# Fused linear attention and squared-ReLU MLP: sums by a product in the first steps, a new order, a last tile in parts

## The chip, the cores and the metric

The kernel runs on one core of a Trainium2 chip. The metric is the time of one execution on the device in microseconds (us); smaller is better. The time before is the median of three runs. A profile is one execution recorded by the hardware profiler; its span runs from the first to the last instruction of the program, and the time of that same execution is a little longer than its span.

Engines: PE is the matrix engine, PEld its weight loads, DVE the vector engine, ACT the scalar engine, POOL the general engine, SP the engine that issues DMAs. "Line" with L and a number is the line of the kernel in the profile of before; the changed kernel has its code eight lines or so further down.

## The reference

Two parts follow each other. The first is a recurrence over 768 positions for 4 batches and 8 heads of 48 columns. The state is a 48x48 matrix for each batch and head.

```python
for t in range(S):
    cur = np.einsum('bhd,bhe->bhde', u[None] * kt, vt)
    y[:, :, t] = np.einsum('bhd,bhde->bhe', rt, state + cur)
    state = wt[:, :, :, None] * state + np.einsum('bhd,bhe->bhde', kt, vt)
```

The second takes the result as 3072 rows of 384 columns and computes `relu(x @ w_in) ** 2 @ w_out`, with 2048 columns in the middle. The output is 3072x384 in float32.

## The kernel before, in words

The 768 positions of a batch are cut into 6 chunks of 128, so there are 24 steps (4 batches of 6 chunks). A step works on all 8 heads, 384 columns, of one chunk. Within a chunk the recurrence becomes products: r is multiplied by the decay up to its position, k by the inverse of the decay, and the products of k and r under a triangular mask replace the loop. Only the state goes from chunk to chunk.

The kernel is written as small functions, one per piece of work, and each has a short name. For step s they are, in the order of the data:

- `ld:s:w`, `ld:s:r`, `ld:s:k`, `ld:s:v` load the chunk (192 KB each, SP, L150).
- `lw` takes the logarithm of w (ACT, L246). `cum` sums it down the chunk by a product with a strict triangle (PE, L272). `ci` makes the inclusive sum with its sign turned, from the exclusive one and lw (DVE, L276). `exp` takes both to the exponent (ACT, L283). `rd` multiplies r and k by them (DVE, L293). The tile of `cum` is in a ring of one buffer (`cp`), which `p` uses too from step 3 on.
- `tr` transposes r and k (PE, L302), `rkt` copies the result to SBUF (DVE or ACT, L187), `p` multiplies k with r (PE, L321), `pm0` and `pm1` mask the two halves (DVE, L333), `ye` multiplies with v into y (PE, L381).
- `su` forms the chunk's own share of the state and the total decay (PE, L347 and L351), `ac` takes the decay's exponent (ACT, L289), `ts` adds the old state (DVE, L356), `sn` applies the decay and gives the new state (DVE or POOL, L190). `ys` multiplies the state with r into y (PE, L370). Where a step has `su` but no `ts`, `sn` reads the product's tile itself. A set `by_product`, empty in this kernel, names steps in which `su` adds the old state by a product with the identity.
- `ku`, `qp`, `q`, `vq` are the term with u (POOL or DVE, L190, with a sum on DVE, L262). `ysb` adds it to y (DVE, L386). `yt` transposes y (PE, L394), `xt` copies it as x to SBUF (ACT or DVE, L187).

`tr`, `su` and `yt` share one buffer (`tr`) in PSUM, so each waits until the copy out of the one before is done.

The second part works on 17 blocks of rows: 0 to 8 of one step (128 rows), 9 to 15 of two steps (256 rows), 16 of one. `m1:i:g` is a group of 12 products (128 columns wide) or 6 products (256 wide) of block i (PE, L412), into a ring of two buffers. `rl` is the ReLU of a group (ACT, L421, or DVE, L423) and `gt` its square: from the ReLU's result by ACT (L433) or DVE (L435), or, with the letter W, by DVE from the PSUM tile and the ReLU (L430), in which case the buffer is free only after `gt`. `m2:i:mt:q` is a quarter of the second product of a 128-row tile (4 products, PE, L454), `os` copies the tile out (L461, L463), `store` writes it (192 KB, SP, L467). The very last tile is split in columns 0 to 255 and 256 to 383 (L450), copied out by `oh` on ACT (L479) and DVE (L480), and written by `sh` with one DMA from ACT's queue (L484) and one from SP's (L485).

The two weights come in four groups each (`ld:g:i`, `ld:g:o`, 768 KB, L176 and L182), and `cast` turns the parts of a group to bfloat16 on ACT, POOL or DVE (L187). `warm` gives PE products on zeros where it has nothing else to do (L473).

What sets the order is a table of words, `ORDER` (lines 16 to 98). The kernel walks it once, and each word issues its instructions. An engine runs its own instructions in exactly that order, and a wait of one holds all behind it on the same engine; a letter at a word's end (A, V, G) names the engine that does it. SP issues the loads and stores in the table's order too. The DMAs finish nearly in the order of issue.

Of the kernel before, what the change touches and what calls it, by code (L numbers as in the profile page):

```python
# [21 lines left out]
warm:1:1 ci:3 vq:2:G yt:0 ysb:1 p:2 exp:3 v:2:V ku:3:G ys:2 pm0:2 xt:0:A warm:1 rd:3 yt:1 cast:i:0:2:A
warm:3:1 qp:3:G xt:1:A pm1:2 cast:i:0:0:A tr:3 q:3 cast:i:0:1:A ye:2 rkt:3:V m1:0:0 cast:i:1:0:G cast:i:1:1:A
ysb:2 m1:1:0 cast:i:1:2:G rl:0:0:A su:2 gt:0:0:W rl:1:0:A ld:4:k p:3 ac:2 pm0:3 cast:i:2:1:G m1:0:1
cast:i:2:2:A ts:2 gt:1:0:A m1:1:1 cast:i:2:0:V sn:2:G rl:0:1:A pm1:3 yt:2 m1:1:2 rl:1:1:V cast:i:3:0:A
cast:i:3:1:G ys:3 gt:0:1:V rl:1:2:A m1:0:2 cast:i:3:2:G gt:1:1:A xt:2:V ld:4:w m1:2:0 rl:0:2:A cast:o:0:2:V
# [5 lines left out]
rl:3:2:A m1:3:3 ld:5:k rkt:4:V gt:3:2:A m2:1:0:2 cast:o:3:0:G cast:o:3:3:A rl:3:3:V ld:6:w cast:o:3:2:A ys:4
cast:o:3:1:G p:4 gt:3:1:V gt:3:3:A m2:0:0:2 ld:7:w pm0:4 lw:5 m2:0:0:3 pm1:4 v:4:G ld:6:r m2:1:0:3 os:0:0:A
vq:4:G cum:5 ye:4 ld:6:k os:1:0:A ci:5 su:4 m2:2:0:0 ac:4 ysb:4 exp:5 ku:5:G ld:8:w ts:4 m2:2:0:1 sn:4:V yt:4
qp:5:G m2:3:0:0 ld:7:r xt:4:A rd:5 m2:2:0:2 store:0:0 q:5 m2:2:0:3 ld:7:k m1:4:0 ld:5:v os:2:0:A lw:6 m1:4:1
rl:4:0:V ld:6:v lw:7 cum:6 tr:5 rl:4:1:A ci:6 m1:4:2 ld:8:r gt:4:0:A rkt:5:V m1:4:3 exp:6 gt:4:1:V ku:6:G
m2:3:0:1 rl:4:2:A rd:6 ld:7:v rl:4:3:A m2:4:0:0 qp:6:G gt:4:2:A p:5 ld:8:v ys:5 gt:4:3:A pm0:5 m2:4:0:1 v:5:A
vq:5:G ld:8:k pm1:5 tr:6 lw:8 q:6 ye:5 cum:7 rkt:6:A ld:9:r m2:4:0:2 ysb:5 ku:7:G ci:7 m2:3:0:2 ld:9:k qp:7:G
exp:7 yt:5 m2:3:0:3 xt:5:V ld:9:w rd:7 v:6:A vq:6:G m1:5:0 os:3:0:A su:6 ld:10:r q:7 rl:5:0:A p:6 m1:5:1 ac:6
pm0:6 gt:5:0:A ld:10:k v:7:G sn:6 m1:5:3 rl:5:1:A pm1:6 vq:7:G ld:10:w tr:7 gt:5:1:A v:8:V m2:5:0:0 rl:5:3:A  # L40
rkt:7:V store:1:0 m1:5:2 ku:8:G gt:5:3:A ld:9:v ye:6 ld:11:r rl:5:2:A cum:8 m2:4:0:3 qp:8:G ysb:6 gt:5:2:A
ci:8 yt:6 ld:11:k m2:5:0:1 ku:9:G xt:6:V exp:8 q:8 ys:7 m1:6:0 ld:10:v lw:9 vq:8:G rd:8 su:7 rl:6:0:A m1:6:1
qp:9:V ac:7 p:7 gt:6:0:A ts:7 ld:12:r m2:5:0:2 rl:6:1:A pm0:7 ku:10:G os:4:0:A m1:6:3 ld:12:k q:9 gt:6:1:A
sn:7:G pm1:7 m1:6:2 rl:6:3:A ld:13:r tr:8 qp:10:G lw:10 gt:6:3:W ye:7 rl:6:2:A cum:9 store:2:0 m2:5:0:3 ysb:7
vq:9:G rkt:8:A store:3:0 ci:9 m2:6:0:0 ld:13:k q:10 gt:6:2:A ys:8 v:9:V yt:7 m2:6:0:1 exp:9 ld:11:w ku:11:V
m2:6:0:2 xt:7:A rd:9 qp:11:G ld:12:w m1:7:0 v:10:A ld:11:v vq:10:G su:8 q:11 rl:7:0:A p:8 m1:7:2 ac:8 pm0:8
gt:7:0:A pm1:8 ku:12:G m1:7:1 ld:14:r os:5:0:A rl:7:2:A ts:8 m2:6:0:3 qp:12:G rl:7:1:V ld:14:k gt:7:2:A cum:10
ye:8 os:6:0:V tr:9 gt:7:1:A sn:8:G store:4:0 ysb:8 m1:7:3 rkt:9:A ld:13:w ci:10 m2:7:0:0 q:12 ld:14:w rl:7:3:A
yt:8 ku:13:V m2:7:0:1 exp:10 gt:7:3:W ld:12:v qp:13:G m2:7:0:2 xt:8:A rd:10 lw:11 m2:7:0:3 ld:15:r q:13 su:9
cum:11 ac:9 m1:8:0 v:11:G ci:11 lw:12 ld:15:k ts:9 m1:8:2 exp:11 vq:11:G os:7:0:V tr:10 rl:8:0:A ld:13:v  # L50
sn:9:G rd:11 ys:9 rkt:10:A m1:8:1 ku:14:V ld:16:r p:9 rl:8:2:A su:10 qp:14:G pm0:9 gt:8:0:A m1:8:3 ld:16:k
pm1:9 ac:10 m2:8:0:0 rl:8:1:A ts:10 ld:15:w gt:8:2:A ye:9 q:14 sn:10:G p:10 gt:8:1:A ysb:9 tr:11 store:5:0
rl:8:3:A pm0:10 ld:16:w m2:8:0:1 vq:12:G lw:13 pm1:10 ld:17:r m2:8:0:2 gt:8:3:A rkt:11:V lw:14 cum:12 ys:10
# [47 lines left out]
def kernel(  # L101
# [11 lines left out]
    nc = tc.nc  # L113
# [414 lines left out]
```

## Time and profile before

| what | value |
| --- | --- |
| time, median of 3 runs | 194.65 us (194.36 to 194.76) |
| the profiled execution | 194.57 us, span 192.8 us |
| PE busy | 183.3 us (95%) |
| DVE busy | 158.5 us (82%) |
| ACT busy | 141.4 us (73%) |
| POOL busy | 80.9 us (42%) |
| memory traffic | 25.17 MB read, 4.72 MB written |
| shares of the chain that ended last | PE 77%, SP's queue 6%, DVE 5%, ACT 4%, DMA 4% |

The chain is followed back from the last instruction, at each step to what released it. Busy time of PE is modelled, since products are pipelined: a product counts as busy until its result is out, so that short waits can lie within it.

### The profile page before, as it was taken

Reading aid. Unit: us, or ns where it says so; the run is one execution under the profiler, and the core shown is the slowest. Engines: PE = TensorE matmul, PEld = TensorE weight load, DVE = VectorE, ACT = ScalarE, POOL = GpSimd, SP = SyncE. Lnnn points to the kernel's source line nnn. Section 1 sums busy time; section 2 is a strip of 40 time slices with the busy share of each in tenths; the row PEclk is TensorE's granted clock in tenths of the full one; section 3 lists DMA queues with packets and bytes.
Section 4 is the critical chain, followed back from the end, with each engine's and each line's share of the span. In section 5 each row is a group of like instructions: output and inputs, shape, how many; then the busy total and the mean of one; then the engine's idle time right before and its main releaser. Section 6 shows DMA issues by size and latency. Waiting matters only on the chain.

```text
span 192.8 us, 5428 instructions
## 1 busy us (share of the span) xinstructions
PE 183.3 (95%) x2171; PEld 138.4 (72%) x2171; DVE 158.5 (82%) x289; ACT 141.4 (73%) x283; POOL 80.9 (42%) x107
## 2 busy tenths in 40 slices
PE   7799699999999999999999999999999999999993
PEld 2345488777777877877778678768768778778772
DVE  4599787987788989899999999998877987877540
ACT  3555689875989989897978666859969858726440
POOL 5287564355397765575366359162141300000000
PEclk9999999999999999999999999999999999999999
DMA  6999998999899999999989899602002000111012
GB/s 133 213 209 274 364 321 194 377 190 219 188 215 185 206 230 183 225 200 233 236 186 216 190 211 226 175 4 82 0 3 82 3 26 19 43 44 41 0 44 82
DMA packets 107180, 30.24 MB, mean 157 GB/s; under 512 B 100370, under 2 KB 105619, under 8 KB 107155
## 3 DMA queue, kind: packets, MB, share of 16 engines
q1 hardware_dynamic: 107010, 29.76, 65.9%
q8 instruction: 17, 0.28, 0.6%
q10 hardware_dynamic: 144, 0.13, 0.2%
q14 instruction: 9, 0.07, 0.1%
HBM read 25.17 MB, written 4.72 MB: 155 GB/s over the span
## 4 chain that ended last, share of the span: by engine, by line
PE 77%; SPq 6%; DVE 5%; ACT 4%; DMA 4%; issue 1%; ACTq 0%
PE m L454 30%; PE m L412 29%; SPq L150 6%; PE tr L302 4%; DMA w_st<-in_moe_w_in_dram 4%; PE cp L321 3%; PE y L381 2%; PE tr L394 2%; PE tr L347 2%; ACT rl L421 2%; PE cp L272 1%; PE y L370 1%; DVE rl L423 1%; PE m L450 1%; DVE gt L435 1%
## 5 line engine op out<-in xcount | busy, mean ns | idle before, releaser
L412 PE MATMUL m<-xT,wi_sb 128*128 128x128 bf16 (+1 forms) x816 | 73.9, 241 | 1.6 <-ACT rl L421 0.3
L454 PE MATMUL m<-wo_sb,gt 128*128 128x384 bf16 x368 | 70.3, 326 | 0.0
L412 PEld LDWEIGHTS <-wi_sb 128*128 128x128 bf16 x816 | 59.8, 97 | 10.0 <-issue 1.7
L421 ACT ACTIVATE rl<-m 128x512 f16<-128x512 f32 x73 | 42.4, 595 | 10.8 <-PE m L412 10.1
L454 PEld LDWEIGHTS <-gt 128*128 128x128 bf16 x368 | 33.4, 97 | 16.9
L433 ACT ACTIVATE gt<-rl 128x512 bf16<-128x512 f16 x57 | 35.3, 631 | 3.8 <-DVE rl L423 3.2
L190 POOL TENSOR_TENSOR qprod<-rk_raw,ku 128x384 f32<-128x384 f32 x23 | 23.5, 1024 | 17.9 <-DVE ku L190 13.1
L333 DVE TENSOR_TENSOR pmT<-cp,tri_strict 128x512 bf16<-128x512 f32 x42 | 27.4, 684 | 4.2 <-PE cp L321 3.9
L293 DVE TENSOR_TENSOR rdec_buf<-rk_raw,cp 128x768 bf16<-128x768 f32 x24 | 22.8, 950 | 3.3 <-ACT cp L283 2.9
L190 POOL TENSOR_TENSOR vq<-v_raw,q 128x384 f32<-128x384 f32 x21 | 17.5, 837 | 13.1 <-DVE y_sb L386 6.5
L283 ACT ACTIVATE cp<-cp 128x768 f32<-128x768 f32 x24 | 19.2, 800 | 3.4 <-DVE cp L276 3.1
L190 POOL TENSOR_TENSOR ku<-rk_raw,u_bc 128x384 f32<-128x384 f32 x17 | 17.3, 1019 | 5.7 <-DMA rk_raw<-in_k_dram 5.7
L423 DVE TENSOR_SCALAR rl<-m 128x512 f16<-128x512 f32 x23 | 15.6, 686 | 3.9 <-PE m L412 3.6
L435 DVE TENSOR_TENSOR gt<-rl 128x512 bf16<-128x512 f16 x34 | 16.3, 481 | 2.9 <-ACT rl L421 2.5
L190 POOL TENSOR_TENSOR S<-t_state,ac_buf 128x384 bf16<-128x384 f32 x12 | 10.2, 848 | 17.1 <-DVE t_state L356 13.1
L276 DVE SCALAR_TENSOR_TENSOR cp<-cp,lw_buf 128x384 f32<-128x384 f32 x24 | 13.4, 559 | 4.2 <-PE cp L272 4.0
L302 PE MATMUL tr<-ident,rdec_buf 128*128 128x128 bf16 x192 | 14.7, 219 | 1.6 <-ACT xT L187 1.2
L461 ACT ACTIVATE o_sb<-m 128x384 f32<-128x384 f32 x18 | 8.8, 488 | 8.1 <-PE m L454 7.4
L386 DVE TENSOR_TENSOR y_sb<-vq,y 128x384 bf16<-128x384 f32 x24 | 13.1, 547 | 1.9 <-PE y L381 1.7
L302 PEld LDWEIGHTS <-rdec_buf 128*128 128x128 bf16 x192 | 12.1, 98 | 3.4 <-issue 1.6
L246 ACT ACTIVATE lw_buf<-w_raw 128x384 bf16<-128x384 f32 x24 | 12.3, 519 | 2.1 <-DMA w_raw<-in_w_dram 1.8
L262 DVE TENSOR_REDUCE q<-qprod 128x8 f32<-128x384 f32 x24 | 13.0, 544 | 0.1
(63 smaller groups left out, 212.9 us busy)
## 6 DMA issues: line engine op xcount, KB each, us to landing
w_raw<-in_w_dram SPq DMA_DIRECT2D x24, 192.0 KB, 3.8
rk_raw<-in_r_dram SPq DMA_DIRECT2D x24, 192.0 KB, 3.8
rk_raw<-in_k_dram SPq DMA_DIRECT2D x24, 192.0 KB, 3.7
v_raw<-in_v_dram SPq DMA_DIRECT2D x24, 192.0 KB, 3.9
out_dram<-o_sb SPq DMA_DIRECT2D x23, 192.0 KB, 2.6
w_st<-in_moe_w_in_dram SPq DMA_DIRECT2D x4, 768.0 KB, 8.7
w_st<-in_moe_w_out_dram SPq DMA_DIRECT2D x4, 768.0 KB, 7.1
out_dram<-o_sb ACTq DMA_DIRECT2D x1, 128.0 KB, 1.9
```

The costliest lines, as they stand in the source:

```text
L190: {"V": nc.vector, "G": nc.gpsimd}[eng].tensor_mul(dst, a, b)
L276: nc.vector.scalar_tensor_tensor(out=cs[:, 1, 0:DM].rearrange("p (h d) -> p h d", h=H), in0=cs[:, 0, 0:DM].rearrange("p (h d) -> p h d", h ...
L283: nc.scalar.activation(cs[:, :, 0:DM], cs[:, :, 0:DM], AF.Exp)
L293: nc.vector.tensor_mul(rdec[:, :, :, 0:D], raw["rk", s][:], tiles.pop(("cs", s))[:, :, 0:DM].rearrange("p a (h d) -> p a h d", h=H))
L302: nc.tensor.transpose(ps_tr[:, i, p, :], rdec[:, i, 2 * p:2 * p + 2, :], ident[:])
L333: nc.vector.tensor_mul(tiles["pmT", s][:, e], tiles["p", s][e].rearrange("p (a t) -> p a t", a=HP), tri_strict[:, None, :].to_broadcast([C ...
L412: nc.tensor.matmul(ps1[:, j, :], wi_sb[:, kk, n * 128:(n + 1) * 128], xT[:, kk, s0 * C:s0 * C + width], start=(kk == 0), stop=(kk == KT - 1))
L421: nc.scalar.activation(rl[:], m1[:], AF.Relu, scale=RS)
L423: nc.vector.tensor_scalar(rl[:], m1[:], RS, 0.0, op0=ALU.mult, op1=ALU.max)
L433: nc.scalar.activation(gt, rl[:], AF.Square)
L435: nc.vector.tensor_mul(gt, rl[:], rl[:])
L454: nc.tensor.matmul(tiles["m2", i, mt][:], gt[:, n, mt * 128:(mt + 1) * 128], wo_sb[:, n, :], start=(n == 0), stop=(n == NT - 1))
```

## The change

- **Sums.** In steps 0, 1 and 2 `cum` makes the inclusive sum by a second product, with a triangle of -1 that has its diagonal (`tri_neg`, built by POOL at the start). The words `ci:0`, `ci:1` and `ci:2` are gone.
- **Old state.** `by_product` is now steps 1 and 2: `su` starts with a product of the identity and the old state, and `ts:1` and `ts:2` are gone; `sn` reads the product's tile.
- **Order.** The table is written anew from the first loads to the end. Other engines do some of the work: of 96 ReLUs DVE does 20 (before 23), of 96 squares DVE does 40 (39; 9 of them from PSUM, before 5), of 24 copies of `rkt` 10 (15), of 23 output copies 12 (5), of 28 casts ACT does 10 (12). Of the 24 `qp` DVE does 5 (1), of the 24 `ku` 5 (7).
- **Fillers.** `warm` uses a zero tile of 128 columns, read four times instead of a tile of 256 read twice; a filler still has 512 columns. There are 32 of them and 5 half ones (35 and 6).
- **Last tile.** Its second half does columns 0 to 255 of all middle rows first and then columns 256 to 383, where before the two parts alternated until the last quarter. Both of its stores go through SP.

The diff without most of the table:

```diff
 ORDER = """
...
-ld:1:k warm:1:1 uc:A v:0:A tr:0 ku:0:V ld:2:k warm:2 qp:0:G lw:1 rkt:0:V ld:1:v cum:1 lw:2 su:0 ci:1 p:0 ac:0
...
-ld:18:r ye:10 ci:12 ku:15:G v:12:A yt:9 m2:8:0:3 ysb:10 xt:9:A ld:14:v exp:12 qp:15:G yt:10 ys:11 xt:10:V
-v:13:A rd:12 m1:9:0 vq:13:G os:8:0:A ld:17:k m1:9:3 q:15 rl:9:0:A ku:16:V tr:12 rl:9:3:A ld:19:r gt:9:0:V p:11
...
+ld:1:k warm:1:1 uc:A v:0:A tr:0 ku:0:V ld:2:k warm:2 qp:0:G lw:1 rkt:0:V ld:1:v cum:1 lw:2 su:0 q:0 p:0 exp:1
...
+m2:8:0:1 ld:17:k ac:10 ci:11 vq:12:G v:12:A m2:8:0:2 ts:10 exp:11 ld:14:v q:15 sn:10:G yt:10 m2:8:0:3 lw:12
+xt:10:V rd:11 ld:15:w m1:9:0 lw:13 m1:9:1 rl:9:0:V vq:13:G cum:12 os:8:0:V tr:11 ld:16:w rl:9:1:A v:13:G ci:12
...
     make_upper_triangular(nc, tri_strict[:], val=1.0, diag=False)
+    tri_neg = consts.tile([C, C], BF16)
+    make_upper_triangular(nc, tri_neg[:], val=-1.0, diag=True)
...
-    warm = consts.tile([C, 256], BF16)
+    warm = consts.tile([C, 128], BF16)
...
+    sum_by_product = frozenset([0, 1, 2])
+
     def cum_(s):
         lw = tiles["lw", s]
         cs = tiles["cs", s] = ps_cp.tile([C, 2, 512], FP32, name="cp")
         nc.tensor.matmul(cs[:, 0, 0:DM], tri_strict[:], lw[:, :, 0:D], start=True, stop=True)
+        if s in sum_by_product:
+            nc.tensor.matmul(cs[:, 1, 0:DM], tri_neg[:], lw[:, :, 0:D], start=True, stop=True)
...
-    by_product = frozenset([])
+    by_product = frozenset([1, 2])
...
-            ns = range(4 * q, 4 * q + 4)
-            for n, (t, lo, hi) in ([(n, x) for n in ns for x in parts] if q < 3 else
-                                   [(n, x) for x in parts for n in ns]):
+            pa, pb = parts
+            todo_n = {2: [(n, pa) for n in range(8, 12)],
+                      3: [(n, pa) for n in range(12, 16)] + [(n, pb) for n in range(8, 16)]}.get(
+                          q, [(n, x) for n in range(4 * q, 4 * q + 4) for x in parts])
+            for n, (t, lo, hi) in todo_n:
...
-        ps = ps_m1.tile([C, 2, 256], FP32, name="m1")
+        ps = ps_m1.tile([C, 4, 128], FP32, name="m1")
...
-        nc.scalar.dma_start(out=out[t0:t0 + C, 0:EA], in_=tiles.pop("oa")[:, 0:EA])
+        nc.sync.dma_start(out=out[t0:t0 + C, 0:EA], in_=tiles.pop("oa")[:, 0:EA])
         nc.sync.dma_start(out=out[t0:t0 + C, EA:DM], in_=tiles.pop("ob")[:, 0:DM - EA])
```

Two places of the new order follow as the engines get it. The first is SP's queue ahead of the first group of the first weight (`w_st`); `w_raw`, `rk_raw` and `v_raw` are the chunk's tiles, and the numbers tell the buffers apart. Before:

```order
L150 DMA v_raw_202<-in_v_dram 128x8x48
L150 DMA v_raw_231<-in_v_dram 128x8x48
L150 DMA w_raw_249<-in_w_dram 128x8x48
L150 DMA rk_raw_253<-in_r_dram 128x8x48
L150 DMA rk_raw_253<-in_k_dram 128x8x48
L176 DMA w_st_262<-in_moe_w_in_dram 128x3x512
```

and in the changed kernel:

```order
L150 DMA v_raw_207<-in_v_dram 128x8x48
L150 DMA v_raw_235<-in_v_dram 128x8x48
L150 DMA w_raw_250<-in_w_dram 128x8x48
L150 DMA v_raw_254<-in_v_dram 128x8x48
L150 DMA rk_raw_269<-in_r_dram 128x8x48
L150 DMA rk_raw_269<-in_k_dram 128x8x48
L176 DMA w_st_314<-in_moe_w_in_dram 128x3x512
```

The load of v of step 3 stood behind five groups of weights; now it stands ahead of all of them. ACT at the same place, where it casts the first weights; `xT` is the copy of x, `wi_sb` the cast weight. Before:

```order
L187 COPY xT_100<-tr_388 128x3x128
L187 CAST wi_sb_98<-w_st_262 128x512
L187 COPY xT_100<-tr_420 128x3x128
L187 CAST wi_sb_98<-w_st_262 128x512 x2
L187 CAST wi_sb_98<-w_st_327 128x512
```

and now:

```order
L187 COPY xT_100<-tr_407 128x3x128
L187 CAST wi_sb_98<-w_st_314 128x512 x2
L187 CAST wi_sb_98<-w_st_339 128x512 x2
L295 ACTIVATE ac_buf2_133<-tr_490 64x4 x2
L427 ACTIVATE rl_535<-m1_502 128x512
```

The copy of x of step 1 is now ahead of the casts and that of step 0 is DVE's; ACT casts two of the three parts of the first group, and POOL the third.

The second place is DVE in steps 1 and 2, where it works without a pause. Numbers with `pmT`'s inputs tell the steps apart. Before, from the mask of step 0 on:

```order
L333 TENSOR_TENSOR pmT<-m_217,tri_strict 128x512
L190 TENSOR_TENSOR S<-tr,ac_buf_124 128x384
L293 TENSOR_TENSOR rdec_buf_132<-rk_raw,cp 128x16x48
L333 TENSOR_TENSOR pmT<-m_218,tri_strict 128x512
L276 SCALAR_TENSOR_TENSOR cp<-cp,lw_buf_122 128x384
L187 COPY rkT<-tr 128x1024
L386 TENSOR_TENSOR y_sb<-vq,y 128x384
L293 TENSOR_TENSOR rdec_buf_134<-rk_raw,cp 128x16x48
```

and now:

```order
L339 TENSOR_TENSOR pmT<-m_224,tri_strict 128x512
L339 TENSOR_TENSOR pmT<-m_225,tri_strict 128x512
L299 TENSOR_TENSOR rdec_buf_137<-rk_raw,cp 128x16x48
L190 TENSOR_TENSOR S<-tr,ac_buf_129 128x384
L392 TENSOR_TENSOR y_sb<-vq,y 128x384
L190 TENSOR_TENSOR ku<-rk_raw,u_bc 128x384
L264 TENSOR_REDUCE q<-qprod 128x8
L190 TENSOR_TENSOR qprod<-rk_raw,ku 128x384
L299 TENSOR_TENSOR rdec_buf_139<-rk_raw,cp 128x16x48
```

Between the `rd` of step 1 (`rdec_buf_132`, now `rdec_buf_137`) and that of step 2 (`rdec_buf_134`, now `rdec_buf_139`) stood four instructions and now stand five others: a mask, `ci` and the copy `rkT` left, and `S`, `ku`, `q` and `qp` of steps 0 to 2 came.

More of the change, by code (lines that the diff above doesn't have):

```diff
@@ L22 @@
[L22 to L26, printed above, removed]
@@ L32 @@
[L32 to L36, printed above, removed]
@@ L37 @@
[L37 to L51, printed above, removed]
@@ new lines @@
+v:9:A vq:9:G m2:5:0:3 pm0:8 rl:7:0:A q:11 lw:11 su:9 m1:7:1 gt:7:0:A pm1:8 ld:11:v m1:7:2 ac:9 ku:12:G
+os:5:0:V rl:7:1:A ld:15:r ts:9 cum:10 ye:8 rl:7:2:A m2:7:0:0 ci:10 qp:12:G v:10:A ld:15:k gt:7:1:V tr:9
+gt:7:2:A sn:9:G m1:7:3 ysb:8 exp:10 store:3:0 vq:10:V m2:7:0:1 store:4:0 rkt:9:A rd:10 ld:16:r m2:6:0:3
+ku:13:G rl:7:3:A m2:7:0:2 q:12 ld:12:v gt:7:3:A qp:13:V yt:8 p:9 xt:8:A m2:7:0:3 q:13 ld:12:w ku:14:G pm0:9
+tr:10 ld:13:w pm1:9 m1:8:0 v:11:A vq:11:G os:7:0:V rkt:10:A m1:8:1 qp:14:G rl:8:0:V ld:13:v ys:9 ye:9 rl:8:1:A
```

130 lines of the change are left out of this document (75 added, 55 removed).

## The prediction

> **What bounds the kernel now.** I read the page's busy shares first, then busy times by stage, then the chain of waits. The first fence is the page's span and its busy shares; in the second each row is a stretch in us with busy times and counts of PE, PEld, DVE, ACT and POOL, then the granted clock, the DMA share and GB/s.
>
> ```profile
> span 192.8 us, 5428 instructions
> PE 183.3 (95%) x2171; PEld 138.4 (72%) x2171; DVE 158.5 (82%) x289; ACT 141.4 (73%) x283; POOL 80.9 (42%) x107
> ```
>
> ```profile
> 0.00:22.60 22.60, 18.05 (x158) 9.32 (x158) 16.78 (x33) 11.82 (x22) 12.73 (x25) 1.00 0.96 229
> 22.60:30.00 7.40, 6.58 (x120) 6.09 (x116) 6.33 (x13) 6.49 (x15) 5.24 (x8) 1.00 1.00 310
> 30.00:80.00 50.00, 49.97 (x681) 39.58 (x679) 43.38 (x79) 43.54 (x90) 29.23 (x36) 1.00 0.97 220
> 80.00:110.00 30.00, 29.16 (x339) 22.15 (x337) 28.34 (x51) 25.83 (x53) 16.30 (x18) 1.00 1.01 210
> 110.00:189.50 79.50, 79.50 (x891) 61.23 (x888) 63.39 (x116) 53.53 (x107) 17.36 (x21) 1.00 0.26 66
> ```
>
> Two regimes stand side by side. To 22.6 us nothing of the MLP can run; the DMAs are at 0.96 of their time, and much of PE's 18.05 us is filler. From 22.6 us on PE is the bound: its idle time is 0.82 us in the second row, 0.03 in the third, 0.84 in the fourth and none in the fifth, together **1.69 us**. That is nearly all that a new order can win after the start; some short waits inside pipelined products add a little to it. So three places can move the time: when the first product of the MLP starts, those 1.69 us, and the 3.3 us after PE's last product.
>
> The chain through the start, with start and length in us and what:
>
> ```profile
> 13.54 7.34 DMA w_st<-in_moe_w_in_dram
> ...
> 20.90 0.62 ACT wi_sb L187
> 21.52 0.38 ACT xT L187
> 21.90 1.04 ACT wi_sb L187 x2
> ...
> 22.99 0.80 PE m L412 x11
> ...
> 24.44 0.69 DVE gt L430
> ```
>
> The first weight group lands at 13.54 + 7.34 = 20.88 us. ACT casts a third of it, then copies x, then casts the rest, and PE's second product begins at 22.99, 2.1 us after the landing.
>
> **Part 1: the first product.** It needs three things: weights, x of step 0, and PE free of what stands ahead of it (`ye:2`). The weights now have one more load of 192 KB ahead of them in SP's queue. The DMAs are full there, at the rate of this row's last column:
>
> ```profile
> 10.00:15.00 5.00, 4.65 (x51) 2.58 (x50) 5.00 (x9) 2.54 (x7) 4.51 (x5) 1.00 1.06 208
> ```
>
> 196.6 KB at 208 GB/s are 0.95 us, so the group lands at about 21.83. Two casts on ACT take 1.04 us by the chain, with 0.1 for starting; POOL does the third at the same time. PE's second product then begins at 21.83 + 1.14 = 22.97. The later load and the split cast cancel: **0.0 us**.
>
> The cover for this is the attention work, which must be done by then. DVE paces it. These rows of the timeline (start, length) are the first four and the last of DVE's 19 instructions from the first mask of step 0 to the second of step 2, and below them PE's `ye:2`:
>
> ```profile
> 10.32 0.68 DVE L333 TENSOR_TENSOR pmT<-m,tri_strict 128x512 bf16<-128x512 f32 x1
> 10.92 0.55 DVE L190 TENSOR_TENSOR S<-tr,ac_buf 128x384 bf16<-128x384 f32 x1
> 11.39 0.95 DVE L293 TENSOR_TENSOR rdec_buf<-rk_raw,cp 128x768 bf16<-128x768 f32 x1
> 12.25 0.69 DVE L333 TENSOR_TENSOR pmT<-m,tri_strict 128x512 bf16<-128x512 f32 x1
> ...
> 20.48 0.68 DVE L333 TENSOR_TENSOR pmT<-m,tri_strict 128x512 bf16<-128x512 f32 x1
> ...
> 22.39 0.36 PE L381 MATMUL y<-v_bf,pmT 128*128 128x48 bf16 x8
> ```
>
> They follow without a gap, 0.60 us apart for a mask, 0.47 for `S` and its like, 0.86 for `rd`, and end at 21.16. The change takes `ci:2`, `ts:1`, `rkt:1` and a cast of v out of that stretch and brings `ku:2`, `qp:2`, a copy of x, `rkt:2` and `sn:1` in. By these spacings the 20 instructions from mask to mask take 5 x 0.60 + 0.68 for the masks, 3 x 0.86 for `rd`, 0.60 for `rkt`, 0.33 for the copy and 9 x 0.47 for the others, 11.4 us. They can begin at about 10.1, so the mask ends near 21.5, or 21.9 with the short waits between DVE and PE that I find when I follow rows and waits by hand. `ye:2` adds its 0.36. That is 0.7 us before 22.97: the removal of `ci` gives no time by itself, since it is paid out again to work moved onto DVE, but it holds.
>
> The second products of `cum` (three of 384 columns) and the identity product of step 1 lie in PE's filler time and cost nothing while there are fillers (32 remain); without that cover they would cost 0.16 us each, an eighth of this row of the chain:
>
> ```profile
> 54.02 1.30 PE m L454 x8
> ```
>
> The identity product of step 2 stands after the first product of the MLP: **+0.16 us**. `tri_neg` delays POOL by two short instructions at the start, before anything needs POOL.
>
> **Part 2: the stage of the weights.** In the chain above `gt` of the first group reads the PSUM tile (L430), which holds one of two buffers until 25.13; PE's third group waits for it. Now that square reads the ReLU's result, and the buffer is free about 0.69 us sooner. ACT also loses two of its 12 casts, the 1.04 us of the chain's row for two. Against it each later weight group lands 0.95 us later too, and the order answers by doing 12 groups of `m1` before the first `m2` instead of 8. Following rows and waits by hand I find short waits on ACT in the new order as well, about as many. Bounds: all 0.82 us won, or 1.0 us lost (one landing later, uncovered). I take **-0.5 us**, nearer the gain because one wait is removed outright.
>
> **Part 3: the long middle.** PE's idle 0.87 us there sits at few places; here are the two largest, first PE waiting for x of step 10 and then PE waiting for a ReLU behind two slow vector instructions.
>
> ```profile
> 87.41 0.31 PE tr L394 x3
> ...
> 87.74 0.37 DVE xT L187
> ...
> 105.66 1.08 DVE gt L435
> 106.75 0.61 DVE rl L423
> ...
> 107.40 0.82 PE m L412 x6
> ```
>
> At the first, only `ys:11` (0.17 us) stood between the transpose and `m1:9:0`; now four products of `m2:8:0:3` (0.65 us) do, which covers the 0.37 us copy. The second belongs to an order that no longer exists. A new order brings its own such places. The engines' sums hardly change: by the counts and mean durations DVE does some 2 us less and ACT some 2 us more of the 158.5 and 141.4. Bounds: -0.87, or +1.0 (as many new waits again). I take **-0.4 us**.
>
> **Part 4: the end.** The last rows of the timeline:
>
> ```profile
> 189.31 0.38 ACT L479 ACTIVATE o_sb<-m 128x256 f32<-128x256 f32 x1 [1.93 <-PE m L450]
> 189.54 0.29 DVE L480 TENSOR_SCALAR o_sb<-y 128x128 f32<-128x128 f32 x1 [3.38 <-PE y L450]
> 189.73 0.41 ACTq L484 DMA_DIRECT2D out_dram<-o_sb  x1
> 189.86 0.33 SPq L485 DMA_DIRECT2D out_dram<-o_sb  x1
> ```
>
> PE's last product ends at the same place, since the same 32 products run. Four short ones (0.055 us each) go behind the last long one, so ACT begins at 189.09 and the first store is issued at 189.51. It now goes through SP and holds it for 0.41 us, to 189.92; the second store, ready at 189.86, waits 0.09 us: **+0.1 us**. If the earlier start of the larger store counts instead, -0.2.
>
> The sum is 0.0 + 0.16 - 0.5 - 0.4 + 0.1 = -0.64 us against the profiled execution's 194.57, 1.77 us of which lie outside its span: **193.9 us**. That execution lies 0.08 us below the median of the runs shown.
>
> **The rivals.**
>
> *The start gets later (slower).* Everything in Part 1 rests on 0.7 us between `ye:2` and the casts. DVE's new stretch has `qp:2` and `ku:2` beside POOL's work. This is what the one such `qp` and the seven `ku` on DVE took (minimum, median, maximum ns):
>
> ```profile
> L190 DVE TENSOR_TENSOR qprod<-rk_raw,ku x1: 1326/1326/1326, 63.7 to 63.7; 128x384 f32<-128x384 f32 x1
> L190 DVE TENSOR_TENSOR ku<-rk_raw,u_bc x7: 545/549/559, 7.6 to 98.8; 128x384 f32<-128x384 f32 x7
> ```
>
> The same shape took 0.55 or 1.33 us. If `qp:2` takes the long time (+0.8) and two hops to PE and back are uncovered (about 0.5 each, for instance from the copy `rkt:2` through `yt`, `ys` and `p` to the mask), the mask ends at 23.7 instead of 21.9, `ye:2` at 24.1, and the first product slips by 1.1 us. It decides as soon as that mask ends after 22.6. With Parts 2 and 3 winning nothing the time is 194.57 + 1.1 + 0.26 = 195.9.
>
> The Trainium skill (GPSIMD Engine Reference, section "Key points") says that POOL shares its SBUF interfaces with DVE, with contention where a DVE instruction has two SBUF inputs. By that rule the four `qp` newly on DVE would each risk the 0.78 us that lies between the two rows, 3.1 us in all, and 197 us if none of it were covered. The trace agrees with it for the one `qp`, but `ku` has two SBUF inputs as well and never was slow, so the rule is only this rival's first 0.8 us, and its chance lies in this rival's.
>
> *Nothing moves (no change).* The weights set the pace of the second stage, each group 0.95 us later, and new small waits replace the old ones: Parts 2 and 3 are nil, 194.57 + 0.26 = 194.8. For it speaks that the DMAs are full to 30 us; against it, that PE waited there for ACT and DVE, not for a landing.
>
> *The order wins nearly all.* The loads and first uses now fit: all of 1.69 us is won, and 0.3 at the start by an earlier landing: 194.57 - 1.99 + 0.26 = 192.8.
>
> **How the numbers follow.** About 0.2%, 0.4 us, can be told from no change here, so faster means below 194.26 and slower above 195.04. Forecast (193.3 to 194.3): 0.42. The order wins nearly all (192.2 to 193.3): 0.15. Nothing moves (194.3 to 195.0): 0.20. The start gets later: 0.23. Faster is 0.42 + 0.15 less a little of its upper edge, 0.55; the same 0.22; slower 0.23. The range runs from 192.2, the lower end of the case that wins nearly all, to 196.0, just past the slower one's worked value, and leaves about a tenth out at each end; the forecast's own range is 193.3 to 194.3.
>
> **What would show it.** Right: PE's first `m1` product with its second at 22.7 to 23.3; the first weight group landing near 21.8; in the stretch from there to 30 us PE idle for under 0.5 us; no wait at the first product of block 9; the last store issued 0.05 to 0.15 us later after PE's end than before. Wrong: DVE's second mask of step 2 ending after 22.6, a `qp` on DVE above 1 us in steps 0 to 2, PE idle above 1 us between 40 and 190, or a landing of the first weights before 21.

## The result and the profile after

The changed kernel takes **192.59 us** (median of 4 runs, 191.86 to 193.03) where the kernel before took 194.7 us beside it. The ratio is 0.9896, with an interval from 0.9861 to 0.9930: faster by 1.4 to 2.7 us. I had forecast 193.9, so the direction holds and the size was too small: the time lies below the forecast's own range (193.3 to 194.3) and inside that of the case "the order wins nearly all" (192.2 to 193.3), which had the smaller chance. A few executions were far slower than the others of their kernel (up to 1031 us) and stand in no ratio; the only profiled one of `w1_square_from_psum` below is among them (233.64 us, at a granted clock of 0.757).

The profiled execution took 193.03 us, the slowest of the four, with a span of 191.2, against 194.57 and 192.8. The page's span and busy shares, then the stages as in the prediction (start, end, length, then busy us and count of PE, PEld, DVE, ACT, POOL, the clock, DMA share, GB/s):

```profile
span 191.2 us, 5444 instructions
PE 183.3 (96%) x2172; PEld 139.1 (73%) x2172; DVE 153.5 (80%) x283; ACT 143.1 (75%) x283; POOL 81.0 (42%) x110
```

```profile
22.60:30.00 7.40, 6.74 (x123) 6.10 (x123) 5.21 (x11) 6.27 (x16) 5.08 (x8) 1.00 0.88 262
30.00:80.00 50.00, 49.98 (x675) 39.63 (x673) 44.23 (x80) 42.88 (x88) 31.44 (x37) 1.00 1.00 232
80.00:110.00 30.00, 30.00 (x362) 23.71 (x360) 28.67 (x54) 25.27 (x52) 13.36 (x17) 1.00 1.04 217
110.00:188.00 78.00, 77.89 (x865) 60.11 (x863) 58.12 (x108) 57.92 (x112) 18.96 (x23) 1.00 0.23 61
```

PE is busy for the same 183.3 us, so by these rows the gain is idle time; that PE's modelled busy time hides a part of it is shown further down. Length less PE's busy time gives the idle time: 0.66 us in the stage of the weights (0.82 before), 0.02 from 30 to 80 (0.03), **0.00 from 80 to 110 (0.84)** and 0.11 after that (none).

The chain through the start (start, length, what) answers to the one of before:

```profile
14.11 7.61 DMA w_st<-in_moe_w_in_dram
...
21.74 1.15 ACT wi_sb L187 x2
...
22.93 0.79 PE m L418 x11
...
24.56 0.71 PE m L418 x12
...
25.29 0.61 ACT rl L427
...
25.92 0.63 ACT gt L439
26.55 0.49 ACT rl L427
27.04 0.51 ACT wi_sb L187
27.54 0.50 ACT rl L427
...
28.95 0.61 ACT rl L427
...
29.60 1.50 PE m L418 x24
```

The first weights land at 14.11 + 7.61 = 21.72 us and PE's second product starts at 22.93 (22.99 before). From 25.3 to 29.6 us the chain runs nearly without a break through ACT: ReLUs, squares, a cast. On this chain ACT is what the stage waits for now.

The terms against the forecast, in us, all from the two profiled executions (spans 192.78 and 191.16 to two decimals). The stage's idle time is counted here from the second product on, so that it is a part of the row above it; the rows from 22.6 us also hold the wait ahead of that product.

| term | forecast | measured |
| --- | --- | --- |
| second product of the MLP | 0.0 | -0.06 (22.99 to 22.93) |
| from there to PE's last end | -0.74 (0.16 - 0.5 - 0.4) | -1.32 (166.51 to 165.19) |
| ... of it PE idle, second product to 30 | -0.5 | -0.28 (0.65 to 0.37) |
| ... of it PE idle, 30 on | -0.4 | -0.74 (0.87 to 0.13) |
| from PE's end to the span's end | +0.1 | -0.24 (3.28 to 3.04) |
| outside the span | 0 | +0.08 (1.79 to 1.87) |
| sum | -0.64 | -1.54 |

### The profile page after: what moved, and what is told of

Same layout as the page of the kernel before. It is cut to its first block, busy times and chain, and to the rows that moved or that the text cites. A ratio compares the mean times of both kernels' runs of the same rounds, so it can differ in the third digit from the quotient of the medians.

```text
span 191.2 us, 5444 instructions
## 1 busy us (share of the span) xinstructions
PE 183.3 (96%) x2172; PEld 139.1 (73%) x2172; DVE 153.5 (80%) x283; ACT 143.1 (75%) x283; POOL 81.0 (42%) x110
## 4 chain that ended last, share of the span: by engine, by line
PE 80%; SPq 7%; ACT 6%; DMA 4%; issue 1%; DVE 0%; ACTq 0%
PE m L462 31%; PE m L418 31%; SPq L150 6%; PE tr L308 5%; DMA w_st<-in_moe_w_in_dram 4%; PE cp L327 3%; ACT rl L427 3%; PE y L387 2%; PE tr L400 2%; PE cp L276 2%; PE y L376 1%; PE tr L353 1%; ACT gt L439 1%; PE m L458 1%; ACT wi_sb L187 1%
## 5 line engine op out<-in xcount | busy, mean ns | idle before, releaser
L418 PE MATMUL m<-xT,wi_sb 128*128 128x128 bf16 (+1 forms) x816 | 74.7, 241 | 1.3 <-ACT wi_sb L187 0.9
L427 ACT ACTIVATE rl<-m 128x512 f16<-128x512 f32 x76 | 44.2, 596 | 13.7 <-PE m L418 12.7
L439 ACT ACTIVATE gt<-rl 128x512 bf16<-128x512 f16 x56 | 34.4, 630 | 1.6 <-DVE rl L429 0.9
L190 POOL TENSOR_TENSOR qprod<-rk_raw,ku 128x384 f32<-128x384 f32 x19 | 19.6, 1033 | 11.4 <-DVE ku L190 5.4
L190 POOL TENSOR_TENSOR ku<-rk_raw,u_bc 128x384 f32<-128x384 f32 x19 | 20.2, 1064 | 0.3 <-issue 0.3
L190 POOL TENSOR_TENSOR S<-t_state,ac_buf 128x384 bf16<-128x384 f32 x11 | 9.4, 853 | 23.3 <-DVE t_state L362 23.3
L441 DVE TENSOR_TENSOR gt<-rl 128x512 bf16<-128x512 f16 x31 | 13.8, 447 | 6.4 <-ACT rl L427 6.3
L187 ACT COPY rkT<-tr 128x1024 bf16<-128x1024 bf16 x14 | 14.2, 1012 | 2.4 <-PE tr L308 2.4
L429 DVE TENSOR_SCALAR rl<-m 128x512 f16<-128x512 f32 x20 | 13.7, 688 | 2.7 <-PE m L418 2.3
L282 DVE SCALAR_TENSOR_TENSOR cp<-cp,lw_buf 128x384 f32<-128x384 f32 x21 | 11.7, 559 | 2.6 <-PE cp L276 2.5
```

What stands on the lines that cost most here:

```text
L187: {"A": nc.scalar.copy, "V": nc.vector.tensor_copy, "G": nc.gpsimd.tensor_copy}[eng](dst, src)
L190: {"V": nc.vector, "G": nc.gpsimd}[eng].tensor_mul(dst, a, b)
L418: nc.tensor.matmul(ps1[:, j, :], wi_sb[:, kk, n * 128:(n + 1) * 128], xT[:, kk, s0 * C:s0 * C + width], start=(kk == 0), stop=(kk == KT - 1))
L427: nc.scalar.activation(rl[:], m1[:], AF.Relu, scale=RS)
L429: nc.vector.tensor_scalar(rl[:], m1[:], RS, 0.0, op0=ALU.mult, op1=ALU.max)
L439: nc.scalar.activation(gt, rl[:], AF.Square)
```

## Experiments

Each time stands beside runs of the kernel before on the same chip, whose medians were 195.08, 194.71 and 195.25 us for the three groups below. An interval of a ratio is some 0.3% wide to each side, 0.6 us; smaller differences are read from the profiles alone.

### Where the gain sits: the tail, the head and the rest taken apart

The changed kernel again, `a0_after`:

> The changed kernel once more, beside the parts of it that follow. It should come out at 192.6 us, 0.99 of the kernel before, like the first time. Only if it lay at 193.5 or above would the gain over my forecast be scatter between chips.

`t1_old_tail` undoes the last two hunks of the change:

```diff
-            todo_n = {2: [(n, pa) for n in range(8, 12)],
-                      3: [(n, pa) for n in range(12, 16)] + [(n, pb) for n in range(8, 16)]}.get(
-                          q, [(n, x) for n in range(4 * q, 4 * q + 4) for x in parts])
+            todo_n = ([(n, x) for n in ns for x in parts] if q < 3 else
+                      [(n, x) for x in parts for n in ns])
...
-        nc.sync.dma_start(out=out[t0:t0 + C, 0:EA], in_=tiles.pop("oa")[:, 0:EA])
+        nc.scalar.dma_start(out=out[t0:t0 + C, 0:EA], in_=tiles.pop("oa")[:, 0:EA])
```

> The changed kernel, but the last tile as before: its two parts alternate until the last quarter, and the first of its stores goes through ACT's queue. By the new trace, where the stretch from PE's last product to the span's end is 0.2 us shorter than before, this kernel takes 0.2 us more than the changed one (192.8). By my forecast's term for the end (+0.1) it takes 0.1 less (192.5). If the last tile is worth nothing, 192.6.

`h1_new_head` joins two tables (the new one up to `ye:4`, then the old words that are left):

```diff
 vq:4:G ld:6:k os:0:0:V cum:5 ye:4
-os:1:0:A ci:5 su:4 ld:5:v m2:2:0:0 ac:4 ysb:4 exp:5 ts:4 m2:3:0:0
+ld:7:w os:1:0:A ci:5 su:4 m2:2:0:0 ac:4 ysb:4 exp:5 ku:5:G ld:8:w ts:4
```

> The new order up to the product with v of step 4 (about 45 us), with the sums and the old state by products; from there the words in their order of before, and the last tile of before. My theory is that the gain sits at the two places of the middle, 80 to 88 and 105 to 107 us, which the old words have: then this kernel gains 0.1 to 0.5 us only (194.1 to 194.6), and waits near 87 and 106 us come back. If the start and the weights' stage carry the gain, it gains 1 us or more (193.6 or less).

`r1_new_rest` is the other way about (the table of before up to the same word, then the new one), without the products:

```diff
-    sum_by_product = frozenset([0, 1, 2])
+    sum_by_product = frozenset([])
-    by_product = frozenset([1, 2])
+    by_product = frozenset([])
```

> The other half: the order of before up to the product with v of step 4, no sums or old state by products, then the new order, and the last tile of before. If the gain sits in the middle: 0.9 to 1.4 us faster than the kernel before (193.2 to 193.7), and PE idle under 0.2 us between 80 and 110 us. If the start carries it: 194.3 or more. If an order gains only as a whole, both halves come out at 194.3 or more.

| kernel | median us | ratio (interval) |
| --- | --- | --- |
| `a0_after` | 192.88 | 0.9900 (0.9868 to 0.9933) |
| `t1_old_tail` | 193.26 | 0.9912 (0.9881 to 0.9944) |
| `h1_new_head` | 194.16 | 0.9955 (0.9925 to 0.9984) |
| `r1_new_rest` | 194.19 | 0.9955 (0.9927 to 0.9983) |

The changed kernel came out as expected, so its gain isn't scatter between chips. The old tail costs 0.4 us by the median; the intervals are wider than that, so only the traces can tell what the tail does (see below).

Each half of the table gives about 0.9 us by the median, so neither my theory (the rest alone) nor its rival (the start alone) holds as it was put. The stage from 80 to 110 us shows which half fills PE's gaps; first `h1_new_head`, then `r1_new_rest`:

```profile
80.00:110.00 30.00, 29.16 (x340) 22.27 (x338) 27.91 (x51) 25.72 (x53) 16.44 (x18) 1.00 0.98 206
```

```profile
80.00:110.00 30.00, 29.47 (x342) 22.66 (x340) 27.77 (x52) 24.72 (x49) 14.71 (x18) 1.00 0.99 206
```

With the old words PE idles the old 0.84 us there. With the new words behind an old head it still idles 0.53, and the chain of waits of `r1_new_rest` says why:

```profile
85.99 3.49 DMA out_dram<-o_sb
...
89.51 0.04 DVE o_sb L470
...
89.98 0.57 DVE cp L282
...
90.57 0.80 ACT cp L289
91.37 0.51 ACT rl L427
...
91.92 0.82 PE m L418 x6
```

DVE's copy of an output tile waits for an earlier store to leave its buffer, and `ci`, the exponent, a ReLU and PE wait behind it. In the changed kernel that copy starts at 87.82 us without a wait. So the seam costs something, and this half may be worth more in place than alone.

What `h1_new_head` gains is less clear: its profile shows only 0.29 us at the second product (22.70 against 22.99), 0.06 us lost from there to PE's end, and a profiled time of 194.4 against 194.57. Its interval reaches down to 0.3 us. More than that isn't shown.

### The products and the order

`p1_products_old_order` keeps table and tail of before and takes only the products in (with them `sn` of steps 1 and 2 goes from POOL to DVE, where the changed kernel has it too):

```diff
+    sum_by_product = frozenset([0, 1, 2])
+    by_product = frozenset([1, 2])
-... ci:0 ... ci:1 ... ci:2 ... ts:1 ... sn:1:G ... ts:2 ... sn:2:G
+... sn:1 ... sn:2
```

> The order and the last tile of before, with the sums of steps 0 to 2 and the old state of steps 1 and 2 by products alone (five vector instructions fewer, five products more). My theory: at the start the weights and ACT's casts decide, so this gives nothing and costs 0.16 to 0.3 us (1.000 to 1.002 of the kernel before; second product of the MLP still near 23.0). If the products carry the gain of the start: 0.995 or less.

`p2_no_products` is the changed kernel without them:

```diff
-exp:0 ... exp:1 ... exp:2 ... sn:1 ... sn:2
+ci:0 exp:0 ... ci:1 exp:1 ... ci:2 exp:2 ... ts:1 sn:1 ... ts:2 sn:2
```

> The changed kernel without those products: the inclusive sums and the old state back on DVE, each straight ahead of what needs it, all else as in the change. My theory: DVE has four more instructions of 0.47 us ahead of the second mask of step 2, which ends at about 23.3 instead of 21.5, PE's first product slips by 0.5 to 0.8 us, and the time is 0.3 to 0.7 us over the changed kernel's. If DVE has that much slack: the mask ends before 22.6 and the time is the changed kernel's.

The products alone: 194.81 us, ratio 0.9993 (0.9961 to 1.0024), no change. In its profiled execution, its fastest of 12, the first product starts at 21.73 and the second 1.2 us earlier than before (21.78 for 22.99). That isn't shown to be the products' doing: in this execution the first weights were there for a cast at 19.65, where the kernel before casts at 20.90. By PE's end 0.7 us of the 1.2 is left (188.80 for 189.50), and by the median nothing. The first cast, the rows of PE, and the chain:

```profile
19.65 0.63 ACT L187 CAST wi_sb<-w_st 128x512 bf16<-128x512 f32 x1
```

```profile
21.73 1.50 PE L418 MATMUL m<-xT,wi_sb 128*128 128x128 bf16 x24
36.21 0.97 PE L461 MATMUL m<-wo_sb,gt 128*128 128x384 bf16 x5 [0.24 <-ACT wo_sb L187]
```

```profile
29.29 5.92 DMA w_st<-in_moe_w_out_dram
```

With eight groups of `m1` done before the first `m2`, PE comes to the second weight's next group when it lands at 29.29 + 5.92 = 35.21 us, and waits for its cast. So my expectation for the time held, but not the one for the second product (near 23.0), at least in this execution: it came early, and the second weight took a part of that back.

The order without the products: 195.51 us, ratio 1.0040 (1.0012 to 1.0068). That is about 2.6 us over the changed kernel by the medians of two groups, 2.4 to 2.8 by the ratios, where I expected 0.3 to 0.7. Step 2's masks (`x2`) on DVE, first in the changed kernel, then in `p2_no_products` with the `S` of step 1 ahead of them:

```profile
20.18 1.29 DVE L339 TENSOR_TENSOR pmT<-m,tri_strict 128x512 bf16<-128x512 f32 x2
```

```profile
20.27 1.19 DVE L190 TENSOR_TENSOR S<-t_state,ac_buf 128x384 bf16<-128x384 f32 x1
...
23.90 1.29 DVE L339 TENSOR_TENSOR pmT<-m,tri_strict 128x512 bf16<-128x512 f32 x2
```

The second mask ends at 25.19 us instead of 21.47, and PE's second product starts at 25.41 instead of 22.93. Four instructions of 0.47 us (`ci:0` to `ci:2`, `ts:1`) are 1.9 of those 3.7 us. Another 0.64 is `S`: 1.19 us where the product form took 0.55, since it now has both inputs in SBUF and started inside an instruction of POOL (more on this below). The rest I put down to the longer way from sum to mask, a hop to DVE and back in each step; no run takes it apart. It begins early: the first mask of step 0 already starts 1.7 us later (11.67 for 9.98). Its profiled execution was 0.7 us slower than its median, so a part of the 3.7 is that run's own.

So neither works alone. Products without the order give nothing, and the order without the products is slower than before by 0.8 us. The five vector instructions that the products remove are what the order spends on DVE.

### The stage of the weights

`s1_v_later` gives the first weight group its old place in SP's queue:

```diff
-ld:3:w ku:1:G ld:3:v rd:1 ... ld:0:i ys:1 ... v:3:G pm1:1 ... cast:i:0:2:G
+ld:3:w ku:1:G rd:1 ... ld:0:i ld:3:v ys:1 ... pm1:1 ... cast:i:0:2:G v:3:G
```

> The changed kernel with v of step 3 loaded (and cast) after the first weight group instead of ahead of it. The first group then lands 0.9 us earlier (20.8 instead of 21.7), and PE's second product begins at about 22.0. If the landing of the first group sets the pace, the time is 0.5 to 0.9 us under the changed kernel's. If the stage is paced by the later groups (the second lands at 23.6 as before) and by ACT's casts and ReLUs, it gains 0.2 us or nothing.

193.26 us, ratio 0.9918 (0.9888 to 0.9948), against 0.9896 to 0.9915 for the changed kernel: no gain over it. PE, then ACT:

```profile
21.96 0.83 PE L418 MATMUL m<-xT,wi_sb 128*128 128x128 bf16 x12
...
24.48 1.70 PE L418 MATMUL m<-xT,wi_sb 128*128 128x128 bf16 x24 [0.16 <-ACT wi_sb L187]
```

```profile
20.38 1.14 ACT L187 CAST wi_sb<-w_st 128x512 bf16<-128x512 f32 x2
23.29 1.14 ACT L187 CAST wi_sb<-w_st 128x512 bf16<-128x512 f32 x2 [1.77 <-DMA w_st<-in_moe_w_in_dram]
```

The first cast starts 1.4 us earlier (20.38 for 21.74) and PE's second product 0.9 us earlier (22.02), but the second group's casts only 0.3 us earlier (23.29 for 23.62), and PE waits for them. What is won at the first group is mostly lost again at the second.

`w1_square_from_psum` gives the first group's square its old form:

```diff
-gt:0:0:V
+gt:0:0:W
```

> The changed kernel, but the square of the first group reads PSUM again, so that its buffer is held until that square ends. By Part 2 of the prediction the third group then waits: PE idle 0.3 to 0.5 us more between 22.6 and 30 us, and the time is 0.2 to 0.5 us over the changed kernel's. If what paces the stage is ACT, the wait is absorbed and the time is the same.

193.29 us, ratio 0.9918 (0.9888 to 0.9949), against 0.9896 to 0.9915 for the changed kernel. The intervals are too wide to tell a cost of 0.2 to 0.5 us from none, and its profile is not read, so this run decides nothing.

The other traces with the same words at the start show something that the two profiled executions above can't. Here is `t2_store_on_act` (described below), ACT and then PE:

```profile
21.21 1.14 ACT L187 CAST wi_sb<-w_st 128x512 bf16<-128x512 f32 x2 [0.69 <-DMA w_st<-in_moe_w_in_dram]
```

```profile
22.40 0.79 PE L418 MATMUL m<-xT,wi_sb 128*128 128x128 bf16 x11 [0.20 <-ACT wi_sb L187]
```

From the first cast to PE's second product it is 22.40 - 21.21 = 1.19 us here, and 1.19 in all six traces with the new head (`after`, `a0_after`, `a1_after`, `t1_old_tail`, `t2_store_on_act`, `h1_new_head`); with the old head it is 2.09 and 2.08 (`before`, `f2_two_swaps`). The way is 0.9 us shorter, every time. What varies is the landing: the first cast starts at 20.90 and 21.11 with the old head, and anywhere from 21.21 to 21.76 with the new one. So the second product comes at 22.40 to 22.95 instead of 22.99 and 23.19, and the profiled execution of the change, with 22.93, is among the late ones. By these eight traces the start gives 0.0 to 0.8 us.

### Single waits, taken away by hand

`f2_two_swaps` is the kernel before with two words moved:

```diff
-lw:12 ld:15:k ts:9 m1:8:2 exp:11 vq:11:G os:7:0:V tr:10 rl:8:0:A
+rl:8:0:A lw:12 ld:15:k ts:9 m1:8:2 exp:11 vq:11:G os:7:0:V tr:10
-gt:10:6:V m1:10:4 qp:19:G rl:10:2:V
+m1:10:4 qp:19:G rl:10:2:V gt:10:6:V
```

> The kernel before with two words of its middle moved: a ReLU of block 8 ahead of a logarithm and an exponent on ACT (PE waits for it 0.33 us near 80 us), and a ReLU of block 10 ahead of a square on DVE (0.5 us near 106 us). By the theory that the waits of the middle are local and add up, PE's idle time between 80 and 110 us falls from 0.84 us to 0.4 or less, and the time by 0.3 to 0.8 us (0.996 to 0.998). If what is put behind is late next, there is no change.

195.34 us, ratio 1.0013 (0.9985 to 1.0040): nothing gained. The stage, then DVE and PE just behind the first moved word:

```profile
80.00:110.00 30.00, 28.70 (x342) 22.08 (x340) 27.54 (x50) 26.37 (x54) 16.55 (x18) 1.00 1.02 214
```

```profile
81.45 0.95 DVE L293 TENSOR_TENSOR rdec_buf<-rk_raw,cp 128x768 bf16<-128x768 f32 x1 [0.92 <-ACT cp L283]
```

```profile
82.46 0.40 PE L321 MATMUL cp<-rkT 64*128 64x128 bf16 x8 [0.83 <-DVE rdec_buf L293]
```

The wait for the ReLU near 80 us (0.17 us of idle time in the kernel before) is gone, but the exponent now comes later, `rd` waits 0.92 us for it, and PE 0.83 us for `rd` and the copy behind it. The other move did better: where PE idled for 0.34 us at 107.40, two waits of 0.10 us are left. PE idles 1.30 us in the stage instead of 0.84.

`b1_fewer_waits` does the same to the changed kernel, and `a1_after` is the changed kernel beside it:

```diff
-cast:i:0:1:A rkt:3:V ... rl:0:0:V ... cast:i:1:0:A
+rkt:3:V cast:i:0:1:V ... rl:0:0:V cast:i:1:0:V
-gt:0:1:A m1:2:1 ts:3 ld:2:o rl:2:0:A
+rl:2:0:A gt:0:1:A m1:2:1 ts:3 ld:2:o
-lw:23 m1:13:7 sn:20:G rl:13:6:A
+m1:13:7 sn:20:G rl:13:6:A lw:23
```

> The changed kernel again, as the measure for the next one on the same chip: 0.990 of the kernel before.

> The changed kernel with four words moved where its trace still shows PE waiting: one cast of the first and one of the second weight group go from ACT to DVE (0.5 us at the first product), a ReLU of block 2 goes ahead of a square on ACT (0.4 us near 29 us), and a logarithm goes behind a ReLU (0.3 us near 151 us). If such waits are local and reach the end, the time is 0.7 to 1.1 us under the changed kernel's. If the landing of the second weight group paces the stage, only the last two count, and it is 0.3 to 0.7 us under. If others come in their place, nothing.

192.97 us (0.9915, 0.9885 to 0.9946) and 193.05 us (0.9900, 0.9871 to 0.9929): the same. PE at the moved ReLU, in the changed kernel and in `b1_fewer_waits` (its profiled execution was its slowest, 194.89 us; only its waits are read):

```profile
29.60 1.50 PE L418 MATMUL m<-xT,wi_sb 128*128 128x128 bf16 x24 [0.28 <-ACT rl L427]
```

```profile
32.38 0.83 PE L418 MATMUL m<-xT,wi_sb 128*128 128x128 bf16 x12 [0.18 <-ACT rl L427]
```

The first ReLU now stands ahead of the square, and PE waits for the next one behind it instead, 0.18 us. At the first product PE waits 0.60 us for DVE's cast where it waited 0.29 for ACT's. Only the moved logarithm left nothing behind: PE's idle time after 110 us is 0.02 us instead of 0.11.

### The tail

`t2_store_on_act` undoes only the last line of the change:

```diff
-        nc.sync.dma_start(out=out[t0:t0 + C, 0:EA], in_=tiles.pop("oa")[:, 0:EA])
+        nc.scalar.dma_start(out=out[t0:t0 + C, 0:EA], in_=tiles.pop("oa")[:, 0:EA])
```

> The changed kernel with the first of the two last stores issued by ACT again; the order of the last products stays new. From PE's last product to the end of the span it took 3.0 to 3.1 us with the new tail and 3.2 to 3.35 with the old one. If the order of the products does it, this kernel takes 3.0 to 3.1; if SP's queue does it, 3.2 or more; by the forecast's term for the end, in which SP holds the second store for 0.09 us, it would be 2.95.

A single execution, 193.37 us. The ends of the changed kernel, of `t1_old_tail` and of `t2_store_on_act`, whose spans are 191.16, 191.47 and 191.60 us (192.78 in the kernel before):

```profile
187.71 0.38 ACT L487 ACTIVATE o_sb<-m 128x256 f32<-128x256 f32 x1 [2.25 <-PE m L458]
188.12 0.33 SPq L492 DMA_DIRECT2D out_dram<-o_sb  x1
188.16 0.29 DVE L488 TENSOR_SCALAR o_sb<-y 128x128 f32<-128x128 f32 x1 [1.77 <-PE y L458]
188.54 0.38 SPq L493 DMA_DIRECT2D out_dram<-o_sb  x1
```

```profile
188.38 0.41 ACTq L491 DMA_DIRECT2D out_dram<-o_sb  x1
188.51 0.33 SPq L492 DMA_DIRECT2D out_dram<-o_sb  x1
```

```profile
188.62 0.37 ACTq L492 DMA_DIRECT2D out_dram<-o_sb  x1
188.97 0.33 SPq L493 DMA_DIRECT2D out_dram<-o_sb  x1
```

From PE's last end to the end of the span it is 3.04 us in the changed kernel, 3.32 in `t1_old_tail`, 2.98 in `t2_store_on_act` and 3.28 in the kernel before. So the new order of the products gives 0.3 us, and SP's queue takes 0.06 of it back: with the first store on ACT the second one is issued 0.03 us after DVE's copy ends (188.94 to 188.97), with both on SP 0.09 us (188.45 to 188.54).

From the issue of the **first**, larger store to the end it is 3.04, 3.09, 2.98 and 3.05 us, nearly the same in all four, and the new order issues it at PE's end (188.12 and 188.62) instead of 0.23 us later. From the second store it is 2.62, 2.96, 2.63 and 2.92 us. Yet it is the second store that lands last. Its row (size, time from issue to landing) in the changed kernel, then in `t1_old_tail`:

```profile
out_dram<-o_sb SPq DMA_DIRECT2D x1, 64.0 KB, 1.6
```

```profile
out_dram<-o_sb SPq DMA_DIRECT2D x1, 64.0 KB, 2.0
```

It lands at 188.54 + 1.6 = 190.14 and 188.51 + 2.0 = 190.51 us, and in the same way at 190.57 in `t2_store_on_act` and 191.76 in the kernel before. The span ends 1.0 us after that landing each time. Issued 0.13 us behind the first store, the second takes 1.9 or 2.0 us; issued 0.35 to 0.42 us behind it, 1.6 us. Either way it lands about 2 us (1.95 to 2.13) after the first one's issue, so most of its own delay is absorbed, and the end follows the issue of the first store. Whether that is for the size of the first store or only for its place isn't tested.

## Why the prediction was right or wrong

**Part 1, the first product: right, and in part by luck.** In the profiled execution the landing was put at 21.83 and came at 21.72, the second product at 22.97 and came at 22.93, the second mask at 21.5 to 21.9 and ended at 21.47. The split cast did what I said: with it the way from the first cast to the second product is 0.9 us shorter in every trace. That the later load cancels it is luck of this one execution. In five others with the same head the second product comes at 22.40 to 22.95, so the term was 0.0 at its worst and -0.8 at its best. That "the removal of `ci` gives no time by itself" is what `p1` shows, and `p2` that without it the attention work isn't done in time. A first product that is early by about 1 us (`p1`, `s1`) gave nothing that the medians show, because the next weight group or the second weight is late next; a late one costs (`p2`).

**Part 2, the stage of the weights: the right wait, too large a size.** The third group waited for the square that held its buffer, and no longer does; the group behind it now starts at 25.94, when ACT's ReLU of the second group has ended (25.89). But in the kernel before that wait was this row:

```profile
25.19 1.50 PE L412 MATMUL m<-xT,wi_sb 128*128 128x128 bf16 x24 [0.16 <-DVE gt L430]
```

That is 0.16 us of idle time, not the 0.69 us by which the buffer is free sooner, nor the 0.5 that I took. From the second product to 30 us PE's idle time fell by 0.28 us (0.65 to 0.37; 0.37 or 0.38 in all six traces with the new head); in the prediction's window, from 22.6 us on, by 0.16. What is left there follows ACT on the chain from 25.3 to 29.6 us, which I had only as a side remark ("short waits on ACT").

**Part 3, the long middle: right mechanism, too small.** I took -0.4 between -0.87 and +1.0; it was -0.74. I expected new places to eat half. With the old words PE idles from 80 to 110 us for 0.84 to 1.30 us (`h1`, `f2`), with the whole new table for none, as in both further runs of the changed kernel. Single words moved off such waits (`f2`, `b1`) gained no time.

**Short waits inside pipelined products** I called "a little". From the second product to PE's end 1.32 us went, although idle time fell by only 1.02 and the identity product (+0.16) came on top: 0.3 to 0.5 us that PE's modelled busy time hides. The starts of PE's products show where. From each interval between two starts I subtracted the median interval of that kind of product. What is left over from the second product on is 7.96 us before and 6.48 now: 1.21 and 1.06 up to 30 us, 1.60 and 1.79 up to 80, **2.84 and 0.96** up to 110, 2.31 and 2.67 after that. (The stages hold somewhat different work in the two kernels, so the total compares better than its parts.) The three waits of the kernel before at 80.71, 88.15 and 107.40 us are 0.33, 0.44 and 0.51 us by the starts, where their idle time is 0.17, 0.28 and 0.34: each is 0.16 us longer than it looks, together 1.28 us for 0.79. The 1.69 us that the prediction took for nearly all that a new order can win leave such parts out.

**Part 4, the end: wrong sign.** The first half held: the first store is issued 0.23 us sooner after PE's end, and SP's queue delays the second. That delay is 0.06 us, the 0.36 us from PE's end to the second store's issue having become 0.42. (So it is by the prediction's own rows too, 189.86 to 189.92; its 0.09 counts from the end of DVE's copy.) The step that failed is that the issue of the second store sets the end. Its landing does, and that follows the first store's issue: -0.24 us instead of +0.1. This was the alternative that I had set aside.

**The rivals.** "The order wins nearly all", worked out at 192.8, came closest. Two thirds of the idle time from the second product on went (1.52 to 0.50 us), with what lay hidden in it. Its gain at the start came about too, by 0.2 to 0.6 us against 22.99 in four of the six traces with the new head, but not by an earlier landing: the weights land later in all six, and the way from them to PE is shorter. "Nothing moves" is excluded by the interval. "The start gets later" didn't happen, but `p2` shows its mechanism with a larger price, from the state's `S` and the hops rather than from `qp`. No `qp` of steps 0 to 2 was slow: the only one there, at 13.95 us, took 0.54 us. The five on DVE took (minimum, median, maximum ns)

```profile
L190 DVE TENSOR_TENSOR qprod<-rk_raw,ku x5: 542/551/824, 14.0 to 90.6; 128x384 f32<-128x384 f32 x5
```

## What to carry to other kernels

When one engine is busy for 95% and the waits sit at a few places, sum the idle time by stage, add what the modelled busy time hides of each wait (here 0.16 us), and take that as the likely gain of a new order that is planned as a whole. A single word moved off a wait can hand the wait to what was put behind, as some of the moves here did; ask what is late next before moving it. Read a start that hangs on a landing in more than one execution: here the landing alone moved by half a microsecond. For the last transfers, look for the landing that the end follows, and for the issue that this landing follows; here these belong to two different stores.

## What the runs showed of the hardware

I had weighed the slow vector instructions and gave them little weight, because `ku` "never was slow". The timelines show what makes them slow, and that this reason was none: not one of those seven `ku` started inside an instruction of POOL, while the one slow `qp` did (63.67, in POOL's `ku` from 63.58 to 64.58). DVE, then POOL, in the kernel before:

```profile
105.64 1.11 DVE L435 TENSOR_TENSOR gt<-rl 128x512 bf16<-128x512 f16 x1
```

```profile
105.47 1.00 POOL L190 TENSOR_TENSOR ku<-rk_raw,u_bc 128x384 f32<-128x384 f32 x1 [0.56 <-DMA rk_raw<-in_k_dram]
```

`gt` reads only SBUF. It started while POOL was at work and ended 0.28 us after POOL's instruction did (106.75 and 106.47), for 1.11 us where its median is 0.42. In the changed kernel a `gt` at 29.58 takes 0.75 us over POOL's instruction from 29.22 to 30.05, again ending 0.28 after it. The `S` of `p2_no_products` that took 1.19 us started at 20.27 while POOL worked from 20.05 on. Of the 34 such squares of the kernel before, 8 started inside an instruction of POOL, and seven of these took 0.57 to 1.11 us (the eighth started 0.13 us before POOL's end); none of the other 26 took more than 0.43. Of the five `qp` on DVE in the changed kernel, the two that started inside an instruction of POOL took 0.82 us, the other three 0.54 to 0.55. Instructions with an input in PSUM don't do this: of the 42 masks that read the tile `cp`, 20 started inside an instruction of POOL in the changed kernel, and all 42 took the same time (minimum, median, maximum ns). So did the six `S` that read the product's tile, four of which started inside one:

```profile
L339 DVE TENSOR_TENSOR pmT<-cp,tri_strict x42: 675/682/692, 24.4 to 170.4; 128x512 bf16<-128x512 f32 x42
```

```profile
L190 DVE TENSOR_TENSOR S<-tr,ac_buf x6: 540/548/551, 12.1 to 135.0; 128x384 bf16<-128x384 f32 x6
```

The Trainium skill (GPSIMD Engine Reference, section "Key points") says that POOL shares its SBUF interfaces with DVE, with contention where a DVE instruction has two SBUF inputs. These rows agree with it; the trace gives the price here, up to 0.7 us for one `gt`. The rows also show a use of the products that I hadn't seen: where `su` adds the old state, `sn` reads PSUM, and it took 0.54 to 0.55 us beside POOL's work and without it.
